# A scan between two dense layers: y of four sequences in one visit, sums on VectorE, scans between w and gT

## Chip, cores, metric

One core of one Trainium2 chip. The metric is the device time of one launch in microseconds, median of repeated launches; all runs used here are in the undisturbed state (granted TensorE clock 0.998 to 1.0). A *ratio* is the mean time of one kernel's fast runs over the mean of the other kernel's fast runs of the same rounds, so it is not quite the ratio of the medians that are quoted.

## The reference

A chunked state-space scan feeds a two-layer network with gate h cos(h):

```python
# batch 4, heads 8, sequence 768, head_dim 32, state 16
for c in range(nc):                          # chunks
    cum = np.cumsum(log_a[chunk])
    L   = np.exp(cum_i - cum_j) * causal
    y   = (C B^T * L) @ x  +  (C @ state) * exp(cum)
    state = decay_full * state + sum_j(B_j x_j * decay_from_j)
x = y.transpose(0, 2, 1, 3).reshape(3072, 256)
h = x @ w_in                                  # 256 -> 2048
out = (h * np.cos(h)) @ w_out                 # 2048 -> 256
```

All of it in fp32. The kernel makes chunks of 128 positions, so there are six (0 to 5), and 16 *turns* per chunk: one turn takes 256 columns of w_in for two of the four sequences, gates the result and multiplies it by w_out.

## The kernel before

Turn n of the loop issues the first product of turn n and the second product of turn n - 2. While chunk c goes through the network, chunk c + 1 is scanned. The parts that matter here:

```python
def first(n):                       # TensorE -> ScalarE -> VectorE
    hp[n] = bank([P, TB], "hp", "h")              # PSUM ring of two
    ... 4 matmuls hp <- w_in, yT ...
    ACT.activation(k, hp[n], AF.Copy, bias=0.25, scale=INV_2PI)
    V.scalar_tensor_tensor(out=w, in0=hp[n], scalar=INV_2PI, in1=k, ...)
def gate(n):   ACT.activation(cos, cos, AF.Sin, ...)
def gated(n):
    V.tensor_tensor(out=gT[n], in0=hp.pop(n), in1=cos, op=ALU.mult)
    differ(n)                                     # three gd on GpSimd

def seven(n):                       # second product, seven matmuls o
    ...                             # on g and gd; two PSUM banks lo, hi
    if j < NJ - 1: return           # every eighth turn:
    ACT.copy(out=ps[:, 0:3], in_=o[c, u][0][:, 0:3])
    V.tensor_copy(out=ps[:, 3:7], in_=o[c, u][1])
    for dst, a_, b_ in (...four adds...):
        G.tensor_tensor(out=dst, in0=a_, in1=b_, op=ALU.add)

# scan of a chunk, for a pair u of two sequences:
#   decays  4 x lam (VectorE scan)   turn2   transposes tp, rT
#   intra2  products g on TensorE    masked  m = g * lam (VectorE)
#   finish2 y = state*rT + xr*m on TensorE, then s_ps, carry
TURN = (NF - 5, NF + 3)             # turns 11 and 19, counted from
                                    # the start of chunk c - 1
for n in range(NC * NF + LAG):
    first(n); turn2 for pairs(n); gate(n); ...; gated(n)
    second(n - LAG)
    intra2, masked  for pairs(n - 1);  masked for pairs(n - 2)
    finish2         for pairs(n - 3)
    decays          for halves_at(n);  reaches for pairs(n + 1)
```

The names in the profile lines: hp is the first product of a turn in PSUM, w its phase and then its cosine, gT the gated result, gd three differences of blocks of gT that the second product o also takes, lam the decays, m the decayed products of the scan. A *y visit* is a stretch in which TensorE leaves the turns for the small matmuls of one scan step (y, then s_ps). A *sum turn* is one that ends an accumulator: ps copies it out of PSUM and four adds make the sums. A chunk is scanned while the chunk before it goes through the network, and a turn number below 16 given for a chunk (turn 2 of chunk 3) counts from the start of that stretch; sum turns are 1 and 9.

Of the kernel before, what the change touches and what calls it, by code (L numbers as in the profile page):

```python
# [8 lines left out]
FP32 = mybir.dt.float32  # L9
# [3 lines left out]
ALU = mybir.AluOpType  # L13
# [12 lines left out]
def kernel(  # L26
# [32 lines left out]
    NB, H, S, D = x.shape  # L59
    N = B.shape[-1]  # L60
    P = 128
    NC = S // P
# [26 lines left out]
    def pair(name):  # L89

        return psum.tile([P, 2, 4 * P], FP32, tag="scan", bufs=2, name=name)
# [142 lines left out]
    unit = const.tile([P, HH, P], FP32, name="unit")  # L234
    G.tensor_copy(out=unit, in_=ident.unsqueeze(1).to_broadcast([P, HH, P]))

    unit0 = const.tile([P, H, W], FP32, name="unit0")
    for t in range(2):
        ts = slice(t * W, (t + 1) * W)
        V.tensor_copy(out=unit0[ts], in_=ident[ts, ts].unsqueeze(1).to_broadcast([W, H, W]))  # L240
# [30 lines left out]
                    axis=mybir.AxisListType.XY, op=ALU.add)  # L271


    a0s = const.tile([P, 2, H, W], FP32, name="a0s")
    halves = a0z.rearrange("p (t i) -> p t i", t=2)
    for h in range(HH):
        ACT.activation(a0s[:, :, h], halves, AF.Copy, scale=mine[:, h:h + 1])
    for t in range(2):
        G.tensor_tensor(out=a0s[:, t, HH:H], in0=halves[:, t:t + 1].to_broadcast([P, HH, W]),
                        in1=mine[:, HH:H].unsqueeze(2).to_broadcast([P, HH, W]), op=ALU.mult)  # L280
    tos = const.tile([P, H, W], FP32, name="tos")
    G.tensor_tensor(out=tos, in0=to.unsqueeze(1).to_broadcast([P, H, W]),
                    in1=mine.unsqueeze(2).to_broadcast([P, H, W]), op=ALU.mult)

# [83 lines left out]
    def intra(b):  # L368
        bT, cT = part[0, b]
        g = [pair("g") for _ in range(2)]  # L370
        for q in range(4):
            r = slice(32 * q, 32 * q + 32)
            PE.matmul(g[q // 2][:, q % 2, 0:2 * P], lhsT=bT[r],
                      rhs=cT[r].rearrange("p t (s i) -> p s t i", s=2), start=True, stop=True)
        l = lam.pop((0, b))
        m = scan.tile([P, 2, H, W], FP32, tag="m", name="m")
        for q in range(2):
            of = [t[:, :, q * HH:(q + 1) * HH].rearrange("p s (k t) i -> p k s (t i)", k=2)
                  for t in (m, l)]
            V.tensor_tensor(out=of[0], in0=g[q][:, :, 0:2 * P].rearrange(  # L380
                "p k (s i) -> p k s i", s=2), in1=of[1], op=ALU.mult)
        part[0, b] = m
# [16 lines left out]
    def turn2(c, u):  # L399
        bc = raw[c][0]  # L400

        tp = pair("tp")[:, 0].rearrange("p (s k i) -> p s k i", s=2, k=2)
        for s in range(2):
            for k in range(2):
                PE.transpose(tp[:, s, k],  # L405
                             bc[:, k, heads(2 * u + s)].rearrange("p h n -> p (h n)"), ident)
        bT = scan.tile([P, 2, P], FP32, tag="bT2", bufs=1, name="bT2")
        ACT.copy(out=bT, in_=tp[:, :, 0])
        cT = scan.tile([P, 2, 2, P], FP32, tag="cT2", bufs=1, name="cT2")
        for t in range(2):  # L410
            ACT.activation(cT[:, :, t], tp[:, :, 1], AF.Copy, scale=slot[:, t:t + 1])
        rT = scan.tile([P, 2, P], FP32, tag="rT", bufs=1, name="rT")
        V.tensor_tensor(out=rT, in0=tp[:, :, 1], in1=reach[c, u], op=ALU.mult)
        part[c, u] = [bT, cT, rT]

# [10 lines left out]
    def masked(c, b):  # L426

        u, s = divmod(b, 2)
        g, ms = part[c, u][0:2]
        l = lam.pop((c, b))  # L430
        m = scan.tile([P, H, P], FP32, tag="m", name="m")
        for q in range(2):
            of = [t[:, q * HH:(q + 1) * HH].rearrange("p (k t) i -> p k (t i)", k=2)
                  for t in (m, l)]
            V.tensor_tensor(out=of[0], in0=g[q][:, :, s * 2 * P:(s + 1) * 2 * P], in1=of[1],  # L435
                            op=ALU.mult)
        ms.append(m)

    def finish2(c, u):
        (_, ms, rT), xr = part.pop((c, u)), raw[c][1]  # L440
        y = pair("y")


        for s in range(2):
            for q in range(4):
                r, p = slice(32 * q, 32 * q + 32), 64 * (q % 2)
                PE.matmul(y[p:p + 64, q // 2, s * P:(s + 1) * P],  # L447
                          lhsT=state[c - 1, u][r, s].rearrange("p t d -> p (t d)"),
                          rhs=rT[r, s], start=(s == 0), stop=False, tile_position=(32 * q, p),
                          skip_group_check=True)  # L450
        for s in range(2):
            for h in range(H):
                q, t = h % 4, h // 4
                PE.matmul(y[32 * q:32 * q + 32, t, s * P:(s + 1) * P], lhsT=xr[:, 2 * u + s, h],  # L454
                          rhs=ms[s][:, h], start=False, stop=True, tile_position=(0, 32 * q),
                          skip_group_check=True)
        if u == 0:
            yT[c] = two.tile([P, 2, TB], FP32, tag="yT", name="yT")
        ACT.copy(out=yT[c][:, :, 2 * u * P:(2 * u + 2) * P], in_=y[:, :, 0:2 * P])
        if c < NC - 1:  # L460
            s_ps = pair("s_ps")[:, 0, 0:4 * D].rearrange("p (s d) -> p s d", s=2)
            for s in range(2):
                sum_up(c, 2 * u + s, s_ps[:, s])
            carry(c, u, s_ps)

    def sum_up(c, b, s_ps):

        xr, sc = raw[c][1], scaled.pop((c, b))
        for q in range(4):
            two_ = slice(2 * q, 2 * q + 2)  # L470
            PE.matmul(s_ps[32 * q:32 * q + 32], lhsT=sc[:, two_].rearrange("p h n -> p (h n)"),
                      rhs=xr[:, b, two_].rearrange("p h d -> p (h d)"), start=True, stop=True,
                      tile_position=(0, 32 * q), skip_group_check=True)
# [51 lines left out]
    def gated(n):  # L525
        cos = turns.pop(n)
        gT[n] = ffn.tile([P, TB], FP32, tag="gT", bufs=LAG + 1, name="gT")
        V.tensor_tensor(out=gT[n], in0=hp.pop(n), in1=cos, op=ALU.mult)  # L528
        gT[n] = gT[n].rearrange("p (q m) -> p q m", q=4)
        if NF <= n < NC * NF - 1:  # L530
            differ(n)
# [49 lines left out]
    def seven(n):  # L581
# [38 lines left out]
        for dst, a_, b_ in ((sum_[:, 0:2], ps[:, 1:3], ps[:, 0:1]),  # L620
                            (sum_[:, 5:7], ps[:, 3:5], sum_[:, 0:1]),
                            (sum_[:, 3:5], ps[:, 5:3:-1], sum_[:, 5:6]),
                            (sum_[:, 2:3], ps[:, 6:7], sum_[:, 6:7])):
            G.tensor_tensor(out=dst, in0=a_, in1=b_.to_broadcast([P, dst.shape[1], P]), op=ALU.add)  # L624
        for s in range(2):
            nc.sync.dma_start(out=to_rows[2 * u + s, c],
                              in_=sum_[s * W:(s + 1) * W, 1:5].rearrange(
# [56 lines left out]
    for dst, src in ((a_cut, cut), (a_all, la)):  # L684
# [13 lines left out]
                 NF + 1: [(0, hind), (1, hind)], NF + 3: [(2, hind), (3, hind)]}  # L698


    TURN = (NF - 5, NF + 3)

    halves_of = {u: [(t - 4 + i, 2 * u + i // 2, i % 2) for i in range(4)]
                 for u, t in enumerate(TURN)}
    ahead = {1: {0: [(4, 0, 0), (6, 0, 1), (8, 1, 0), (9, 1, 1)]}}

    sums = {}

# [18 lines left out]

    def pairs(n):

        at = [(1 + (n - t) // NF, u) for u, t in enumerate(TURN) if (n - t) % NF == 0]  # L730
        return [(c, u) for c, u in at if 0 < c < NC]

    def halves_at(n):
        return [(c, b, t) for c in range(1, NC) for u in range(2)
                for m, b, t in ahead.get(c, {}).get(u, halves_of[u]) if m + (c - 1) * NF == n]

    EARLY = 3
    rest_of_loads()
    for n in range(NC * NF + LAG):
        c, f = divmod(n, NF)  # L740
        early = n < EARLY
        if n < NC * NF:
            if f == 0 and c > 0:
                load(c + 2)
            first(n)
            if n == 0:
                first_scan()
            for at in pairs(n):
                turn2(*at)
            rests = [grade(*piece[m], later=True)  # L750
                     for m in ((n,) if early else ()) + ((n + 1,) if n >= EARLY - 1 else ())
                     if m in piece]
            gate(n)
            for rest in rests:
                if rest:
                    rest()
            if not early and n in piece:
                join(*piece[n])
            gated(n)
            if early and n in piece:  # L760
                join(*piece[n])
            if n in (1, 2):
                carry(0, n - 1, sums[n - 1])
        for i, js in differ_at.get(n, ()):
            differ_w(i, js)
        if n >= LAG:
            second(n - LAG)
        for c, u in pairs(n - 1):
            intra2(c, u)
            masked(c, 2 * u)  # L770
        for c, u in pairs(n - 2):
            masked(c, 2 * u + 1)
        for c, u in pairs(n - 3):
            finish2(c, u)
            if u == 1:
                raw.pop(c)
        for c, b, t in halves_at(n):
            decays(c, b, t)
            if t == 1:
                load_a(c + 1, (b,))  # L780
        for c, u in pairs(n + 1):
            for b in (2 * u, 2 * u + 1):
                reaches(c, b)
                load_along(c + 1, (b,))
# [30 lines left out]
```

## Time and profile before

| | before |
|---|---|
| time, median | 386.46 us (386.18 to 387.12) |
| span of the profiled run | 384.9 us |
| busy: TensorE, VectorE, GpSimd, ScalarE | 98, 69, 64, 45% |
| from hp of turn 24 to hp of turn 40 (16 turns, one chunk) | 60.61 us |
| turn without scan work | 3.29 us |

The lines of the profile that the argument rests on stand in the prediction below.

### The profile page before, as it was taken

To read this page: it belongs to the slowest core of one execution; us is meant where nothing else is said; L and a number is where in the kernel's file an instruction comes from. 1 tells how busy PE (TensorE), PEld (TensorE's weight loads), DVE (VectorE), ACT (ScalarE), POOL (GpSimd) and SP (SyncE) were. 2 spreads that over 40 slices of the span, in tenths; PEclk is the share of its full clock that TensorE was granted. 3 is DMA by queue.
4 is the path that set the end of the run, shared out by engine and by line. 5 is a ranking of instruction groups with operands and counts; after the bars stand their busy time and mean duration, and the time that the engine had idled before them with its cause. 6 is when DMAs were issued, how large, how long until landed. Compare 5 with 4: busy or idle time off the path is not lost.

```text
span 384.9 us, 7726 instructions
## 1 busy us (share of the span) xinstructions
PE 378.3 (98%) x2982; PEld 331.2 (86%) x2982; DVE 265.9 (69%) x395; ACT 172.9 (45%) x303; POOL 245.4 (64%) x366
## 2 busy tenths in 40 slices
PE   8999999999999999999999999999999999999996
PEld 3578887888899899899899899899899989989995
DVE  7879999678667658657657757756765865863443
ACT  3878566534334334335334434434433433433441
POOL 5757665458859549648648837855955855853751
PEclk9999999999999999999999999999999999999999
DMA  7989899975002951301791301201210000010001
GB/s 83 270 235 266 249 230 137 181 96 151 2 0 63 148 52 57 96 2 54 127 81 55 97 2 56 81 17 43 68 43 1 21 10 0 2 27 3 7 22 27
DMA packets 106371, 30.42 MB, mean 79 GB/s; under 512 B 75520, under 2 KB 102240, under 8 KB 106336
## 3 DMA queue, kind: packets, MB, share of 16 engines
q1 hardware_dynamic: 106176, 29.81, 38.9%
q8 instruction: 23, 0.38, 0.5%
q10 hardware_dynamic: 160, 0.13, 0.1%
q14 instruction: 12, 0.10, 0.1%
HBM read 26.59 MB, written 3.34 MB: 78 GB/s over the span
## 4 chain that ended last, share of the span: by engine, by line
PE 82%; DVE 7%; POOL 3%; ACT 2%; issue 2%; DMA 2%; SPq 1%; ACTq 0%
PE hp L512 37%; PE o L609 32%; PE g L422 3%; PE y L454 3%; DVE mag L209 2%; DVE w L518 2%; DMA xr<-in_x_dram 2%; PE y L447 2%; DVE lam L344 2%; PE o L571 1%; DVE gT L528 1%; PE warm L101 1%; ACT w L523 1%; PE a_ps L298 1%; PE tp L405 1%
## 5 line engine op out<-in xcount | busy, mean ns | idle before, releaser
L512 PE MATMUL hp<-yT,w_in 128*128 128x256 f32 x768 | 184.4, 383 | 0.6 <-POOL w_in L217 0.3
L512 PEld LDWEIGHTS hp<-yT,w_in 128*128 128x128 f32 x768 | 139.2, 190 | 22.7 <-issue 4.5
L553 POOL TENSOR_TENSOR gd<-gT 128x256 f32<-128x256 f32 x79 | 71.9, 911 | 89.5 <-DVE gT L528 86.2
L528 DVE TENSOR_TENSOR gT<-hp,w 128x512 f32<-128x512 f32 x96 | 66.3, 691 | 69.9 <-ACT w L523 60.1
L523 ACT ACTIVATE w<-w,quarter 128x512 f32<-128x512 f32 x96 | 69.3, 722 | 97.2 <-DVE w L518 97.2
L516 ACT ACTIVATE k<-hp 128x512 int32<-128x512 f32 x96 | 57.1, 595 | 90.8 <-PE hp L512 90.7
L518 DVE SCALAR_TENSOR_TENSOR w<-hp,k 128x512 f32<-128x512 f32 x96 | 65.4, 681 | 36.7 <-ACT k L516 36.4
L609 PE MATMUL o<-words,gd 128*128 128x128 f32 x474 | 67.0, 277 | 0.6 <-POOL gd L555 0.6
L609 PEld LDWEIGHTS o<-words,gd 128*128 128x128 f32 x474 | 59.3, 192 | 2.4 <-POOL gd L555 2.2
L344 DVE TENSOR_TENSOR_SCAN lam<-arow,unit 128x512 f32<-128x512 f32 x40 | 55.7, 1394 | 0.0
L609 PEld LDWEIGHTS o<-w_out,gT 128*128 128x128 f32 x316 | 46.9, 191 | 3.6
L609 PE MATMUL o<-w_out,gT 128*128 128x128 f32 x316 | 48.0, 274 | 0.0
L555 POOL TENSOR_TENSOR gd<-gT,gd 128x128 f32<-128x128 f32 x79 | 43.1, 546 | 6.2
L556 POOL TENSOR_TENSOR gd<-gT,gd 128x128 f32<-128x128 f32 x79 | 35.9, 455 | 6.2
L571 PE MATMUL o<-w_out,gT 128*128 128x256 f32 x128 | 30.3, 380 | 0.4 <-POOL w_out L217 0.4
L609 PE MATMUL o<-w_out,gd 128*128 128x128 f32 x158 | 30.6, 275 | 0.0
L609 PE MATMUL o<-words,gT 128*128 128x128 f32 x158 | 30.5, 275 | 0.0
L571 PEld LDWEIGHTS o<-w_out,gT 128*128 128x128 f32 x128 | 24.2, 190 | 4.0 <-POOL w_out L217 0.8
L435 DVE TENSOR_TENSOR m<-g,lam 128x512 f32<-128x512 f32 x40 | 25.6, 681 | 0.0
L624 POOL TENSOR_TENSOR sum<-ps,sum 128x256 f32<-128x256 f32 (+1 forms) x27 | 24.2, 909 | 1.4
L609 PEld LDWEIGHTS o<-w_out,gd 128*128 128x128 f32 x158 | 24.0, 192 | 0.0
L609 PEld LDWEIGHTS o<-words,gT 128*128 128x128 f32 x158 | 24.0, 192 | 0.0
(91 smaller groups left out, 293.9 us busy)
## 6 DMA issues: line engine op xcount, KB each, us to landing
arow<-a_cut SPq DMA_DIRECT2D x20, 512.0 KB
words<-in_moe_w_in_dram SPq DMA_DIRECT2D x8, 512.0 KB
words<-in_moe_w_out_dram SPq DMA_DIRECT2D x8, 512.0 KB
out_dram<-sum SPq DMA_DIRECT2D x18, 128.0 KB
xr<-in_x_dram SPq DMA_DIRECT2D x4, 512.0 KB
along<-a_all SPq DMA_DIRECT2D x20, 64.0 KB
xr<-in_x_dram SPq DMA_DIRECT2D x8, 128.0 KB
bc<-in_B_dram SPq DMA_DIRECT2D x4, 256.0 KB
```

The source lines that it names most:

```text
L344: V.tensor_tensor_scan(out=lam[c, b][:, hs].rearrange("p h i -> p (h i)"), data0=rows_.rearrange("p h i -> p (h i)"), data1=unit.rearrange ...
L435: V.tensor_tensor(out=of[0], in0=g[q][:, :, s * 2 * P:(s + 1) * 2 * P], in1=of[1], op=ALU.mult)
L512: PE.matmul(to_[:, e], lhsT=w_in[:, k, fs], rhs=y[:, k, u], start=(k == 0), stop=(k == KT - 1), skip_group_check=True)
L516: ACT.activation(k, hp[n], AF.Copy, bias=0.25, scale=INV_2PI)
L518: V.scalar_tensor_tensor(out=w, in0=hp[n], scalar=INV_2PI, in1=k, op0=ALU.mult, op1=ALU.subtract)
L523: ACT.activation(cos, cos, AF.Sin, bias=quarter, scale=TWO_PI)
L528: V.tensor_tensor(out=gT[n], in0=hp.pop(n), in1=cos, op=ALU.mult)
L553: G.tensor_tensor(out=d[:, 0:2], in0=g[:, 1:2].to_broadcast([P, 2, P]), in1=g[:, 3::-3], op=ALU.subtract)
L555: G.tensor_tensor(out=d[:, 2], in0=g[:, 0], in1=d[:, 0], op=ALU.subtract)
L556: G.tensor_tensor(out=d[:, 3], in0=g[:, 2], in1=d[:, 2], op=ALU.subtract)
L571: PE.matmul(o[c, u][:, t], lhsT=g[:, 2 * e + t], rhs=w_out[:, 2 * j + e], start=(j == e == t == 0), stop=(j == NJ - 1 and e == 1), skip_gr ...
L609: PE.matmul(at[q], lhsT=a_[q], rhs=w[q], start=(j == 0 and q in starts), stop=(j == NJ - 1), skip_group_check=True)
```

## The change

The intent: (1) for chunks 2 to 5 compute y of all four sequences in one visit to TensorE instead of two; (2) take the four sums of a finished accumulator from GpSimd to VectorE; (3) issue scans (and the second m of a pair) between w and gT, where VectorE waits for the cosine. Larger buffer rings for m and rT make (1) possible; two setup tiles were put into the m ring to pay for it.

```diff
-    def finish2(c, u):
+    def finish2(c, us):                      # us = (0, 1) for chunks 2 to 5
+        parts = [(2*u + s, part[c,u][1][s], part[c,u][2][:, s]) for u in us for s in range(2)]
         y = pair("y")
-        for s in range(2):                   # state part, then m part
+        for i, (b, _, rT) in enumerate(parts):
 ...
-            G.tensor_tensor(out=dst, in0=a_, in1=b_..., op=ALU.add)
+            V.tensor_tensor(out=dst, in0=a_, in1=b_..., op=ALU.add)
 ...
-    TURN = (NF - 5, NF + 3)
+    late = [((0,), {0: 11}, [(4,0,0), (6,0,1), (8,1,0), (9,1,1)], 14),
+            ((1,), {1: NF + 2}, [(NF - 2 + i, 2 + i//2, i % 2) for i in range(4)], NF + 5)]
+    at_once = (0, 1), {0: 7, 1: 11}, 14      # transposes in turns 7, 11; y after 14
+    halves_of = {2: [(2,0,0), (3,0,1), (5,1,0), (6,1,1), (7,2,0), (8,2,1), (10,3,0), (11,3,1)]}
+    each = [(i - 1, i // 2, i % 2) for i in range(2 * NB)]   # scans in turns -1 to 6
 ...
+            behind = [halved(...) for halves_at(n)]
+            behind = [masked(c, 2u + 1) for pairs(n - 2)] + behind
+            if n not in piece and behind:    # from turn 16 on
+                behind.pop(0)()              # between w and gT
             gated(n)
+            for do in behind:
+                do()
```

More of the change, by code (lines that the diff above doesn't have):

```diff
@@ L235 @@
     G.tensor_copy(out=unit, in_=ident.unsqueeze(1).to_broadcast([P, HH, P]))
-    unit0 = const.tile([P, H, W], FP32, name="unit0")
+    both = scan.tile([P, 2, H, W], FP32, tag="m", bufs=4, name="both")
+    unit0, tos = both[:, 0], both[:, 1]
     for t in range(2):
@@ L271 @@
                     axis=mybir.AxisListType.XY, op=ALU.add)
-    a0s = const.tile([P, 2, H, W], FP32, name="a0s")
+    a0s = scan.tile([P, 2, H, W], FP32, tag="m", bufs=4, name="a0s")
     halves = a0z.rearrange("p (t i) -> p t i", t=2)
@@ L280 @@
                         in1=mine[:, HH:H].unsqueeze(2).to_broadcast([P, HH, W]), op=ALU.mult)
-    tos = const.tile([P, H, W], FP32, name="tos")
     G.tensor_tensor(out=tos, in0=to.unsqueeze(1).to_broadcast([P, H, W]),
@@ L375, in intra @@
         l = lam.pop((0, b))
-        m = scan.tile([P, 2, H, W], FP32, tag="m", name="m")
+        m = scan.tile([P, 2, H, W], FP32, tag="m", bufs=4, name="m")
         for q in range(2):
@@ L411, in turn2 @@
             ACT.activation(cT[:, :, t], tp[:, :, 1], AF.Copy, scale=slot[:, t:t + 1])
-        rT = scan.tile([P, 2, P], FP32, tag="rT", bufs=1, name="rT")
+        rT = scan.tile([P, 2, P], FP32, tag="rT", name="rT")
         V.tensor_tensor(out=rT, in0=tp[:, :, 1], in1=reach[c, u], op=ALU.mult)
@@ L430, in masked @@
         l = lam.pop((c, b))
-        m = scan.tile([P, H, P], FP32, tag="m", name="m")
+        m = scan.tile([P, H, P], FP32, tag="m", bufs=4, name="m")
         for q in range(2):
@@ L437, in masked @@
         ms.append(m)
-    def finish2(c, u):
-        (_, ms, rT), xr = part.pop((c, u)), raw[c][1]
+    def finish2(c, us):
+        xr = raw[c][1]
+        parts = [(2 * u + s, part[c, u][1][s], part[c, u][2][:, s]) for u in us for s in range(2)]
         y = pair("y")
-        for s in range(2):
+        for i, (b, _, rT) in enumerate(parts):
             for q in range(4):
                 r, p = slice(32 * q, 32 * q + 32), 64 * (q % 2)
-                PE.matmul(y[p:p + 64, q // 2, s * P:(s + 1) * P],
-                          lhsT=state[c - 1, u][r, s].rearrange("p t d -> p (t d)"),
-                          rhs=rT[r, s], start=(s == 0), stop=False, tile_position=(32 * q, p),
+                PE.matmul(y[p:p + 64, q // 2, i * P:(i + 1) * P],
+                          lhsT=state[c - 1, b // 2][r, b % 2].rearrange("p t d -> p (t d)"),
+                          rhs=rT[r], start=(i == 0), stop=False, tile_position=(32 * q, p),
@@ L450, in finish2 @@
                           skip_group_check=True)
-        for s in range(2):
+        for i, (b, m, _) in enumerate(parts):
             for h in range(H):
                 q, t = h % 4, h // 4
-                PE.matmul(y[32 * q:32 * q + 32, t, s * P:(s + 1) * P], lhsT=xr[:, 2 * u + s, h],
-                          rhs=ms[s][:, h], start=False, stop=True, tile_position=(0, 32 * q),
+                PE.matmul(y[32 * q:32 * q + 32, t, i * P:(i + 1) * P], lhsT=xr[:, b, h],
+                          rhs=m[:, h], start=False, stop=True, tile_position=(0, 32 * q),
@@ L456, in finish2 @@
                           skip_group_check=True)
-        if u == 0:
-            yT[c] = two.tile([P, 2, TB], FP32, tag="yT", name="yT")
-        ACT.copy(out=yT[c][:, :, 2 * u * P:(2 * u + 2) * P], in_=y[:, :, 0:2 * P])
+        s_ps = pair("s_ps")[:, 0].rearrange("p (u s d) -> p u s d", u=2, s=2)
+        for i, u in enumerate(us):
+            del part[c, u]
+            if u == 0:
+                yT[c] = two.tile([P, 2, TB], FP32, tag="yT", name="yT")
+            ACT.copy(out=yT[c][:, :, 2 * u * P:(2 * u + 2) * P],
+                     in_=y[:, :, 2 * i * P:(2 * i + 2) * P])
+            for s in range(2 if c < NC - 1 else 0):
+                sum_up(c, 2 * u + s, s_ps[:, u, s, 0:2 * D])
@@ L460, in finish2 @@
         if c < NC - 1:
-            s_ps = pair("s_ps")[:, 0, 0:4 * D].rearrange("p (s d) -> p s d", s=2)
-            for s in range(2):
-                sum_up(c, 2 * u + s, s_ps[:, s])
-            carry(c, u, s_ps)
+            for u in us:
+                carry(c, u, s_ps[:, u, :, 0:2 * D])
     def sum_up(c, b, s_ps):
@@ L623, in seven @@
                             (sum_[:, 2:3], ps[:, 6:7], sum_[:, 6:7])):
-            G.tensor_tensor(out=dst, in0=a_, in1=b_.to_broadcast([P, dst.shape[1], P]), op=ALU.add)
+            V.tensor_tensor(out=dst, in0=a_, in1=b_.to_broadcast([P, dst.shape[1], P]), op=ALU.add)
         for s in range(2):
@@ L698 @@
                  NF + 1: [(0, hind), (1, hind)], NF + 3: [(2, hind), (3, hind)]}
-    TURN = (NF - 5, NF + 3)
-    halves_of = {u: [(t - 4 + i, 2 * u + i // 2, i % 2) for i in range(4)]
-                 for u, t in enumerate(TURN)}
-    ahead = {1: {0: [(4, 0, 0), (6, 0, 1), (8, 1, 0), (9, 1, 1)]}}
+    late = [((0,), {0: 11}, [(4, 0, 0), (6, 0, 1), (8, 1, 0), (9, 1, 1)], 14),
+            ((1,), {1: NF + 2}, [(NF - 2 + i, 2 + i // 2, i % 2) for i in range(4)], NF + 5)]
+    at_once = (0, 1), {0: 7, 1: 11}, 14
+    halves_of = {2: [(2, 0, 0), (3, 0, 1), (5, 1, 0), (6, 1, 1), (7, 2, 0), (8, 2, 1), (10, 3, 0),
+                     (11, 3, 1)]}
+    each = [(i - 1, i // 2, i % 2) for i in range(2 * NB)]
+    plan = [(c, NF * (c - 1), *v) for c in range(1, NC) for v in (
+        late if c == 1 else [(*at_once[:2], halves_of.get(c, each), at_once[2])])]
     sums = {}
@@ L728, in pairs, with halved, ends @@
     def pairs(n):
-        at = [(1 + (n - t) // NF, u) for u, t in enumerate(TURN) if (n - t) % NF == 0]
-        return [(c, u) for c, u in at if 0 < c < NC]
+        return [(c, u) for c, at, _, turn_at, _, _ in plan for u in turn_at
+                if at + turn_at[u] == n]
     def halves_at(n):
-        return [(c, b, t) for c in range(1, NC) for u in range(2)
-                for m, b, t in ahead.get(c, {}).get(u, halves_of[u]) if m + (c - 1) * NF == n]
+        return [(c, *h) for c, at, _, _, halves_of, _ in plan for m, *h in halves_of if at + m == n]
+    def halved(c, b, t):
+        decays(c, b, t)
+        if t == 1:
+            load_a(c + 1, (b,))
+    def ends(n):
+        return [(c, us) for c, at, us, _, _, end in plan if at + end == n]
     EARLY = 3
@@ L758 @@
                 join(*piece[n])
+            behind = [lambda at=at: halved(*at) for at in halves_at(n)]
+            behind = [lambda at=(c, 2 * u + 1): masked(*at) for c, u in pairs(n - 2)] + behind
+            if n not in piece and behind:
+                behind.pop(0)()
             gated(n)
+            for do in behind:
+                do()
             if early and n in piece:
@@ L770 @@
             masked(c, 2 * u)
-        for c, u in pairs(n - 2):
-            masked(c, 2 * u + 1)
-        for c, u in pairs(n - 3):
-            finish2(c, u)
-            if u == 1:
+        for c, us in ends(n):
+            finish2(c, us)
+            if 1 in us:
                 raw.pop(c)
-        for c, b, t in halves_at(n):
-            decays(c, b, t)
-            if t == 1:
-                load_a(c + 1, (b,))
         for c, u in pairs(n + 1):
```

## The prediction

> **What bounds the kernel now.** I read the page's totals first, then the waits, then the order of time around one stage.
>
> ```profile
> span 384.9 us, 7726 instructions
> PE 378.3 (98%) x2982; PEld 331.2 (86%) x2982; DVE 265.9 (69%) x395; ACT 172.9 (45%) x303; POOL 245.4 (64%) x366
> PE 82%; DVE 7%; POOL 3%; ACT 2%; issue 2%; DMA 2%; SPq 1%; ACTq 0%
> ```
>
> TensorE sets the time. VectorE and GpSimd have a third of the span free; they matter only where TensorE waits for them. So I ask what TensorE's queue loses. The waits, with who waited, for whom, the total, the count and the longest:
>
> ```profile
> PEld o L609 <- POOL gd L555: 2.2, 9, 0.8
> PEld hp L512 <- issue: 4.5, 14, 0.6
> PEld y L454 <- issue: 1.7, 10, 0.2
> PEld o L609 <- DVE ps L619: 0.2, 1, 0.2
> ```
>
> In order of time, the starts of single matmuls lie on a fixed grid: a quiet turn (hp, then the seven products o) takes 1.73 + 1.56 = 3.29 us and repeats to 0.01 us. Off the grid after 90 us are only (a) the scan visits, (b) eight waits of 0.25 to 0.31 us (2.06 in all, a 0.10 us slow restart included) for a difference gd of GpSimd, each in the o three turns after the sums begin to be made, (c) one such wait of 0.82 us at 94 us behind GpSimd's weight differences, (d) one of 0.28 us at 209 us for VectorE's copy of an accumulator. (b) in chunk 3, from the timeline (start, length):
>
> ```profile
> 181.19 2.87 POOL L624 TENSOR_TENSOR sum<-ps,sum 128x256 f32<-128x256 f32 x3
> 181.68 1.32 DVE L344 TENSOR_TENSOR_SCAN lam<-arow,unit 128x512 f32<-128x512 f32 x1
> 184.02 0.84 POOL L553 TENSOR_TENSOR gd<-gT 128x256 f32<-128x256 f32 x1
> 185.45 0.74 PEld L609 LDWEIGHTS o<-words,gd 128*128 128x128 f32 x6 [0.18 <-POOL gd L555]
> ```
>
> The sums keep GpSimd until 184.02, gd comes late, and TensorE waits at 185.45. A y visit, ten of which exist:
>
> ```profile
> 194.30 0.39 PE L609 MATMUL o<-w_out,gd 128*128 128x128 f32 x2
> 194.62 0.67 PE L447 MATMUL y<-rT,state 32*64 32x128 f32 x16
> 195.21 1.08 PE L454 MATMUL y<-m,xr 128*32 128x128 f32 x32
> 196.11 0.41 PE L471 MATMUL s_ps<-xr,sc 128*32 128x64 f32 x16
> 196.44 0.48 PE L512 MATMUL hp<-yT,w_in 128*128 128x256 f32 x1
> ```
>
> And a quiet turn of VectorE with a scan after gT:
>
> ```profile
> 199.17 0.69 DVE L518 SCALAR_TENSOR_TENSOR w<-hp,k 128x512 f32<-128x512 f32 x1 [2.11 <-ACT k L516]
> 200.72 0.69 DVE L528 TENSOR_TENSOR gT<-hp,w 128x512 f32<-128x512 f32 x1 [0.86 <-ACT w L523]
> 201.32 1.22 DVE L344 TENSOR_TENSOR_SCAN lam<-arow,unit 128x512 f32<-128x512 f32 x1
> 201.55 1.51 POOL L553 TENSOR_TENSOR gd<-gT 128x256 f32<-128x256 f32 x1 [3.11 <-DVE gT L528]
> ```
>
> VectorE idles 0.86 us between w and gT, waiting for ScalarE's cosine; gd takes 1.51 us beside the scan, 0.73 elsewhere.
>
> **What the Trainium skill says.** "Perfetto Trace Analysis", Identifying the Most-Contended Engine, warns that matmul busy time does not show how near TensorE is to its limit, and names weight-load time and MFU instead; so I use starts, not the 98%. "TensorEngine Tiling (Array Packing)", Key Properties: switching the tiling mode drains the array. The trace agrees: 205 ns from the last o to the first y against 112 within o, 198 ns from the row-tiled to the column-tiled part against 109 within each, 320 ns between the first two hp afterwards against 216. "SBUF — State Buffer", Who interferes with whom: a VectorE instruction with two SBUF inputs and a GpSimd instruction that reads SBUF exclude each other. The trace agrees (gd 0.73 alone, 1.51 beside a scan); copies and products that read PSUM, such as ps and m, leave gd at 0.73.
>
> **The change part by part.**
>
> (1) One y visit instead of two for chunks 2 to 5. Streaming is kept: groups of four small matmuls every 109 ns (y) and 56 ns (s_ps). Saved is what one visit pays apart from its groups, read from single starts: entry 205 - 112 = 93; first state group 161 - 109 = 52; switch 217 - 109 = 108; first group of the m part 133 - 109 = 24; end of s_ps 169 - 56 = 113; slow second hp 320 - 216 = 104. Sum 0.49 us; four times, 1.98 us off the path. The transposes (tp) and g are still two visits. Chunk 1 keeps its two y visits, because its data come during chunk 0.
>
> (2) The sums go to VectorE. GpSimd loses 9 x (0.73 + 2.87) = 32 us, off the path apart from the eight waits: -2.06 us. VectorE gains 9 x four adds. It has the same forms at the end of the kernel: 0.425 us for 128x256, 0.293 for 128x128, with some 0.03 between dependent ones: 3 x 0.46 + 0.33 = 1.7 us, 15 us in all. Since they have two SBUF inputs, they alternate with the three gd of the turn. With w at 2.62 us after the start of its hp, gT at 4.17 to 4.41 and ps 0.6 later, I get the end of the sums at 7.4 to 7.65 us after that hp. The next w would start at 5.9, so it is 1.5 to 1.7 late.
>
> (3) A scan between w and gT. w issues in 0.60, the scan takes some 1.15, so gT starts 1.75 to 1.8 us after w in place of 1.55: 0.25 later, but GpSimd's gd no longer collides with the scan. TensorE needs gT two turns on, when hp's bank is reused: 6.58 us after hp in quiet turns, gT now ending at 4.86. The slack is 1.72 us, so most turns cost nothing.
>
> (4) Two places where this slack is used up. Where a sum turn also has a scan or a product m before gT (7 of 9), ps ends near 5.69 in place of 5.45; TensorE writes the second of the two accumulator banks again at 5.69. With 0.05 for the semaphore and 0.10 for the restart that is 0.15 us, 7 times: +1.05 us. In the turn after a sum, where there is a scan too (chunks 3 to 5, turn 2, three times), gT ends near 4.15 + 1.75 + 0.69 = 6.6 against 6.58: about 0.16 each, +0.48 us. Where transposes lie in between (turn 10) the limit is 7.02 and nothing is lost.
>
> (5) Moves. In chunk 1 the second half's transposes come a turn earlier, and its g lies before the o that waited at 94 us: GpSimd has 1.43 us more there. I expect this wait (0.82) gone, and the one at 209 us (0.28) too, or counted among the seven of (4). The larger rings for m and rT and the two setup tiles put into the m ring change no wait on the path: up to turn 13 the order on every engine is the same, so the first 70 us should be equal, the 0.4 us wait at 60.5 included.
>
> Sum: -1.98 - 2.06 - 0.82 - 0.28 + 1.05 + 0.48 = -3.61 us. The median before is 386.46, so **382.8 us**, 0.9% less; the span near 381.3.
>
> **The rivals.** *VectorE becomes the bound in places.* For it: in chunks 2 to 5 all scans, products and sums fall into some eleven turns, where a turn holds w 0.6, scan 1.15, gT 0.6 and often 1.2 to 1.7 more, against 3.29; the two tightest turns have a margin of nothing. Against it: the backlog of a sum is worked off at 0.9 us a turn in the turns after. If each of 18 sums and reach turns missed by 0.2 us, it would cost 3.6 us: about 386.4, the whole gain. *The wait for gd stays,* because VectorE's sums block GpSimd in place of its own: for it, 1.51 against 0.73 us; against it, the three gd need 1.4 us and alternate with the sums, ending near 7.0 us after hp against a need of 6.58 + 1.73 + 0.45 = 8.76 for the second. It would leave 384.9. *Everything works and the restarts of (4) don't come:* 386.46 - 5.14 = 381.3. *The y visit saves nothing* because the matmuls wait for the last m: against it, the last m is made in turn 13 and the visit follows turn 14; this would give 384.8.
>
> **Range and chances.** 381.3 is the floor of what I can find, and 384.8 the sum with one of the two large terms lost. I take **381.3 to 384.8**. Faster by over 2% would need 7.7 us, more than all waits on the path: 0.02. Slower by over 2% would need steady stalls of VectorE, 0.1 us in every turn and more: 0.02. Within 2%: 0.96.
>
> **What would show it.** Right: six y visits instead of ten, a merged one some 3.5 us from its first y to the next hp; no wait of o for gd L555; GpSimd busy 245 - 32 = 213 us or less, VectorE near 266 + 15 = 281; gd about 0.73 in most turns; scans of chunks 2 to 5 in the idle time before gT; small waits of o for the copy ps about every 8 turns. Wrong: waits of hp for gT in turns 2, 3, 10 or 11 of the chunks, longer than 0.2 us; a lasting wait for gd; or a start (first 70 us) that differs, which I took as equal.

## The result

| | before | changed |
|---|---|---|
| time, median | 386.79 us (386.18 to 387.15, 4 runs) | 382.71 us (382.49 to 383.33, 4 runs) |
| ratio, 95% interval | | 0.9899 (0.988 to 0.9918) |
| span of the profiled run | 384.9 us | 381.3 us |
| period, turn 24 to 40 | 60.61 us | 60.04 us |

Later the same changed kernel gave 0.9906 and 0.9921. The gain is about 1%. The totals of the changed kernel's page (busy time, share, instructions):

```profile
span 381.3 us, 7681 instructions
PE 375.1 (98%) x2982; PEld 330.9 (87%) x2982; DVE 279.1 (73%) x431; ACT 172.2 (45%) x303; POOL 213.5 (56%) x330
```

VectorE has 13 us more, GpSimd 32 us less, TensorE the same instructions. In the changed kernel's waits no o waits for a gd any more; GpSimd idles longer before its first gd instead (103.5 us in all, 89.5 before), and TensorE waits for none of that:

```profile
POOL gd L560 <- DVE gT L535: 74.3, 48, 4.6
POOL gd L560 <- PE hp L519: 25.4, 13, 3.0
```

The joined y visit of the changed kernel (lines are 7 lower in its text, so y is L450 and L457):

```profile
134.37 0.39 PE L616 MATMUL o<-w_out,gd 128*128 128x128 f32 x2
134.69 1.10 PE L450 MATMUL y<-rT,state 32*64 32x128 f32 x32
135.72 1.95 PE L457 MATMUL y<-m,xr 128*32 128x128 f32 x64
137.49 0.63 PE L478 MATMUL s_ps<-xr,sc 128*32 128x64 f32 x32
138.05 0.91 PE L519 MATMUL hp<-yT,w_in 128*128 128x256 f32 x3
```

From first y to hp it takes 3.36 us; by single starts the single visit before took 1.83, twice 3.66. With the entry (0.09) and the slow second hp (0.10), which are outside these numbers, the difference is 0.49 us.

And a turn of the changed kernel that has both a scan and the sums (turn 33), with the turn after it:

```profile
147.35 0.69 DVE L525 SCALAR_TENSOR_TENSOR w<-hp,k 128x512 f32<-128x512 f32 x1 [0.64 <-ACT k L523]
147.96 1.24 DVE L345 TENSOR_TENSOR_SCAN lam<-arow,unit 128x512 f32<-128x512 f32 x1
149.12 0.66 DVE L535 TENSOR_TENSOR gT<-hp,w 128x512 f32<-128x512 f32 x1
149.70 0.67 DVE L626 COPY ps<-o 128x512 f32<-128x512 f32 x1
150.30 0.63 DVE L631 TENSOR_TENSOR sum<-ps 128x256 f32<-128x256 f32 x1
150.96 1.36 DVE L631 TENSOR_TENSOR sum<-ps,sum 128x256 f32<-128x256 f32 x3
152.25 0.68 DVE L525 SCALAR_TENSOR_TENSOR w<-hp,k 128x512 f32<-128x512 f32 x1
152.85 1.21 DVE L345 TENSOR_TENSOR_SCAN lam<-arow,unit 128x512 f32<-128x512 f32 x1
153.98 0.66 DVE L535 TENSOR_TENSOR gT<-hp,w 128x512 f32<-128x512 f32 x1
154.78 0.89 PE L519 MATMUL hp<-yT,w_in 128*128 128x256 f32 x3
```

VectorE has no pause from 147.35 to the second gT. hp of turn 33 starts at 144.73, so ps ends at 144.73 + 5.64 and the sums at 144.73 + 7.6; the second gT ends at 154.64 and hp of turn 36, which uses its bank again, starts at 154.78, 0.07 off the grid. This is the place where the slack is used up. The other kind of place is a sum turn in which VectorE has a product m or a scan before gT (here turn 25, in which two m run until 117.48):

```profile
118.00 0.68 DVE L626 COPY ps<-o 128x512 f32<-128x512 f32 x1
118.44 1.00 PE L616 MATMUL o<-words,gd 128*128 128x128 f32 x6
```

The copy of the accumulator ends at 118.68 and the first o that writes this bank again starts at 118.73, so that these six matmuls take 1.00 us where they take 0.83 on the grid.

### The profile page after: what moved, and what is told of

Same layout as the page of the kernel before. It is cut to its first block, busy times and chain, and to the rows that moved or that the text cites. A ratio compares the mean times of both kernels' runs of the same rounds, so it can differ in the third digit from the quotient of the medians.

```text
span 381.3 us, 7681 instructions
## 1 busy us (share of the span) xinstructions
PE 375.1 (98%) x2982; PEld 330.9 (87%) x2982; DVE 279.1 (73%) x431; ACT 172.2 (45%) x303; POOL 213.5 (56%) x330
## 4 chain that ended last, share of the span: by engine, by line
PE 87%; DVE 6%; ACT 2%; issue 2%; POOL 1%; ACTq 0%
PE hp L519 40%; PE o L616 33%; PE g L423 3%; PE o L578 3%; PE y L457 3%; DVE mag L209 2%; PE y L450 1%; DVE w L525 1%; DVE gT L535 1%; PE warm L101 1%; DVE mag L207 1%; PE tp L406 1%; PE a_ps L299 1%; ACT w L530 1%; DVE lam L345 1%
## 5 line engine op out<-in xcount | busy, mean ns | idle before, releaser
L560 POOL TENSOR_TENSOR gd<-gT 128x256 f32<-128x256 f32 x79 | 59.4, 752 | 103.5 <-DVE gT L535 74.3
L535 DVE TENSOR_TENSOR gT<-hp,w 128x512 f32<-128x512 f32 x96 | 65.1, 678 | 33.3 <-ACT w L530 30.7
L563 POOL TENSOR_TENSOR gd<-gT,gd 128x128 f32<-128x128 f32 x79 | 46.0, 582 | 6.2
L562 POOL TENSOR_TENSOR gd<-gT,gd 128x128 f32<-128x128 f32 x79 | 42.7, 541 | 6.2
L328 POOL TENSOR_TENSOR sc<-bc,lam 128x128 f32<-128x128 f32 x20 | 8.5, 431 | 14.7 <-DVE lam L345 7.3
```

The costliest lines, as they stand in the source:

```text
L560: G.tensor_tensor(out=d[:, 0:2], in0=g[:, 1:2].to_broadcast([P, 2, P]), in1=g[:, 3::-3], op=ALU.subtract)
L562: G.tensor_tensor(out=d[:, 2], in0=g[:, 0], in1=d[:, 0], op=ALU.subtract)
L563: G.tensor_tensor(out=d[:, 3], in0=g[:, 2], in1=d[:, 2], op=ALU.subtract)
```

## The experiments

Each kernel was compared with the kernel before on the same chip in five rounds. *Period* is from hp of turn 24 to hp of turn 40, and from 40 to 56 and 56 to 72, where they differ.

| kernel | ratio to before | period, us |
|---|---|---|
| before | 1 | 60.61, 60.96, 60.61 |
| changed (three measurements) | 0.9899, 0.9906, 0.9921 | 60.04 |
| a1 changed, sums on GpSimd | 1.0007 | 61.91, 61.70, 60.74 |
| a2 before, sums on VectorE | 1.0078 | 61.29 |
| a3b changed, scans behind sums | 1.0064 | 62.51, 61.24, 61.25 |
| a4 two visits, turns 13 and 14 | 1.0029 | 61.19 |
| a4b two visits, turns 14 and 15 | 0.9971 | 60.52 |
| a5 chunk 1 a turn later | 0.9944 | 60.04 |
| b1 free sum turns, first try | 0.9889 | 59.77 |
| c1 free sum turns | 0.9879, 0.9868 | 59.62 |

**a0: the changed kernel again**, no edit.

> The changed kernel itself once more, as the measure for the others of this call: about 382.7 us, span 380.5 to 381.3, waits of TensorE after 90 us about 1.4 us in all.

383.06 us (382.76 to 383.36), ratio 0.9906, span 380.7 us: as expected. A third measurement beside a5 and c1:

> The changed kernel as the measure for these two: period 60.04 us, ratio to the kernel before near 0.990.

383.51 us, ratio 0.9921 (0.9908 to 0.9935), period 60.05. The three ratios differ by 0.002 for one and the same kernel, so ratios of different calls should not be compared below that; the period can.

**a1: the sums alone back on GpSimd.**

```diff
-            V.tensor_tensor(out=dst, in0=a_, ...
+            G.tensor_tensor(out=dst, in0=a_, ...
```

> The changed kernel with the four sums back on GpSimd, all else kept. Theory 1 (the sums' own place is worth the 2.06 us that I credited to it): the eight waits of o for gd come back, the waits of hp for gT in turn 2 (0.43 us) go: 1.6 us more than the changed kernel, about 384.3. Rival (gd was late because sums, gd and scans excluded each other, and the scans' new place before gT alone frees GpSimd): no wait for gd, or only in turn 10 where the two reach scans still collide (up to 4 times 0.25): between 0.5 less and 0.5 more than the changed kernel.

386.89 us, ratio 1.0007 (0.999 to 1.0024): the whole gain is gone, 3.8 us, over twice what theory 1 had said. The rival falls, and so does the size. The trace shows why; GpSimd and TensorE of a1 from turn 34 on:

```profile
152.46 0.72 POOL L631 TENSOR_TENSOR sum<-ps 128x256 f32<-128x256 f32 x1
153.26 2.87 POOL L631 TENSOR_TENSOR sum<-ps,sum 128x256 f32<-128x256 f32 x3
154.44 1.44 DVE L345 TENSOR_TENSOR_SCAN lam<-arow,unit 128x512 f32<-128x512 f32 x1
156.09 0.41 POOL L328 TENSOR_TENSOR sc<-bc,lam 128x128 f32<-128x128 f32 x1
156.46 0.72 POOL L560 TENSOR_TENSOR gd<-gT 128x256 f32<-128x256 f32 x1
157.77 0.74 PEld L616 LDWEIGHTS o<-words,gd 128*128 128x128 f32 x6 [1.13 <-POOL gd L562]
157.80 1.39 POOL L563 TENSOR_TENSOR gd<-gT,gd 128x128 f32<-128x128 f32 x1
159.24 0.30 PEld L616 LDWEIGHTS o<-w_out,gd 128*128 128x128 f32 x2 [0.51 <-POOL gd L563]
```

With a scan before gT in every turn from -1 to 6, the sums on GpSimd meet a scan, the sc product and the next scan. gd of turn 34 starts at 156.46, 3.6 us after its gT was done (152.83), and o waits twice. That chunk loses 1.9 us (period 61.91 against 60.04), the next 1.7 and the third 0.7; from first hp to last matmul a1 takes 4.2 us longer than a0. So with the sums on GpSimd, o waits 2.06 us for gd in the old order of turns, but 4.6 us in the new one (both with restarts).

**a2: the kernel before with nothing but the sums moved.**

```diff
-            G.tensor_tensor(out=dst, in0=a_, ...      # before.py
+            V.tensor_tensor(out=dst, in0=a_, ...
```

> The kernel before with nothing changed but the four sums on VectorE. If the sums' place were worth its 2.06 us by itself: 2.06 us less than before, about 384.7. Theory now (the parts depend on each other: here the scan stands behind the sums in the sum turn, so w of the next turn comes 1.9 us later and gT passes the limit of 7.02 us after hp): waits of hp for gT of about 0.5 us and of o for gd of about 0.5 us in each half chunk, 5 us more than before rather than less.

389.3 us, ratio 1.0078 (1.0064 to 1.0092): 3.0 us slower, 2.5 to 3.6 by the interval, and 2.4 us from first hp to last matmul in the traces. The eight waits for gd after the sums are gone, as my sum has it, but a wait of hp for gT takes the place of each. VectorE and TensorE of a2:

```profile
148.43 1.36 DVE L624 TENSOR_TENSOR sum<-ps,sum 128x256 f32<-128x256 f32 x3
149.71 1.21 DVE L344 TENSOR_TENSOR_SCAN lam<-arow,unit 128x512 f32<-128x512 f32 x1
150.84 0.66 DVE L518 SCALAR_TENSOR_TENSOR w<-hp,k 128x512 f32<-128x512 f32 x1
152.37 0.69 DVE L528 TENSOR_TENSOR gT<-hp,w 128x512 f32<-128x512 f32 x1 [0.86 <-ACT w L523]
153.20 1.10 PE L512 MATMUL hp<-yT,w_in 128*128 128x256 f32 x4 [0.35 <-DVE gT L528]
```

Sums and then a scan stand in front of the next w; VectorE afterwards idles 0.86 us for the cosine, and gT is late for hp. Each costs 0.59 us with the restart against 0.25 saved; eight times 0.34, less the 0.28 us wait for ps that went too, is the 2.4 us of the traces. The wait that I expected for gd did not come, so it is not 5. The same move that carries the change loses time when done alone.

**a3b: scans and second m behind the sums.**

```diff
-            if n not in piece and behind:
-                behind.pop(0)()
             gated(n)
-            for do in behind: do()
 ...
             second(n - LAG)
+        for do in behind: do()
```

> The changed kernel with the scans and second m products behind gT, the copy ps and the sums, where the kernel before has them. Theory (VectorE's order in a turn decides): the waits for ps go (1.0 us), but in turns 2 and 10 gT ends near 7.5 us after its hp against limits of 6.58 and 7.02: about 1 us in turn 2 of chunks 3 to 5 and 0.5 us in turn 10, in all 3 to 5 us more than the changed kernel, 386 to 388. Rival (VectorE is idle for over a quarter of the span, its order inside a turn does not matter; what helped was only to relieve GpSimd): within 0.5 us of the changed kernel.

388.76 us, ratio 1.0064 (1.0051 to 1.0077). Lines of VectorE and TensorE from the sums of turn 33 on:

```profile
152.63 1.36 DVE L631 TENSOR_TENSOR sum<-ps,sum 128x256 f32<-128x256 f32 x3
153.91 1.21 DVE L345 TENSOR_TENSOR_SCAN lam<-arow,unit 128x512 f32<-128x512 f32 x1
155.04 0.66 DVE L525 SCALAR_TENSOR_TENSOR w<-hp,k 128x512 f32<-128x512 f32 x1
156.57 0.69 DVE L535 TENSOR_TENSOR gT<-hp,w 128x512 f32<-128x512 f32 x1 [0.86 <-ACT w L530]
157.41 0.89 PE L519 MATMUL hp<-yT,w_in 128*128 128x256 f32 x3 [0.72 <-DVE gT L535]
```

It is some 6 us more than the changed kernel by the ratios (1.0064 - 0.9906) and by the trace (6.1 us more from first hp to last matmul): the theory's mechanism, but more than its 3 to 5 us. hp waits 0.89 us for gT after turn 2 and 0.60 after turn 10, where 1 and 0.5 were expected. What my figure left out are single waits around chunk 2, where the scans of two chunks meet: two y visits that waited 0.65 and 0.49 us, an o that waited 0.7 us for the accumulators' copies, and one more late gT (0.74). VectorE was busy 72% here, no more than in the changed kernel; its order inside a turn decides.

**a4 and a4b: two y visits again.** First after turns 13 and 14:

```diff
-        return [(c, us) for c, at, us, _, _, end in plan if at + end == n]
+        return [(c, (u,)) for c, at, us, _, _, end in plan for u in us
+                if at + end - us[-1] + u == n]
```

> The changed kernel with the y visit of chunks 2 to 5 made twice again (sequences 0 and 1 after turn 13, 2 and 3 after turn 14), same streaming. Theory (a visit has a fixed price of 0.49 us on TensorE, from single starts): 1.98 us more, about 384.7. Rival (the gain came from elsewhere, joining is neutral): within 0.3 us of the changed kernel.

387.85 us, ratio 1.0029: more than either theory. The first visit waited 0.67 us in each chunk, because y takes the PSUM buffer that the last m products read:

```profile
130.91 1.28 DVE L436 TENSOR_TENSOR m<-g,lam 128x512 f32<-128x512 f32 x2
131.74 0.67 PE L450 MATMUL y<-rT,state 32*64 32x128 f32 x16 [0.60 <-DVE m L436]
```

So this experiment measured two things at once. The second try puts the visits after turns 14 and 15 (`us[0]` for `us[-1]`):

> Two y visits for chunks 2 to 5 once more, now after turns 14 and 15, because in the first try the first visit waited 0.67 us per chunk for a PSUM buffer still read by the last m. Theory (fixed price of a visit 0.49 us): the period from hp of turn 24 to hp of turn 40 is 60.04 + 0.49 = 60.53 us and the time 2.0 us over the changed kernel, 384.7 to 385.0. Rival (the visit's price was only that wait): period within 0.1 us of 60.04.

385.2 us (384.72 to 385.84), ratio 0.9971 (0.9959 to 0.9984). The period is 60.52 us, 0.48 over the changed kernel, where 0.49 was expected. A visit has a fixed price; from turn 24 to turn 88 nothing else changed, and four chunks make 1.9 us. At the very end a4b has 0.37 us more, where the last o waits for the last gT (a4 has this too); why that gT came later was not traced.

**a5: the second half of chunk 1 a turn later**, as before the change.

```diff
-            ((1,), {1: NF + 2}, [(NF - 2 + i, ...)], NF + 5)]
+            ((1,), {1: NF + 3}, [(NF - 1 + i, ...)], NF + 6)]
```

> The changed kernel with the second half of chunk 1 a turn later throughout (scans 15 to 18, transposes after hp of turn 19, g after turn 20, y after turn 22), as in the kernel before. Theory (step 5: the wait of 0.82 us at 94 us went because g now lies ahead of the o that waited): the wait for gd in turn 20 comes back, 0.8 us more between hp of turn 14 and hp of turn 24 than in the changed kernel, apart from the moved visits. Rival (it went because scans ahead of gT leave GpSimd free for its weight differences): no wait there, or under 0.2 us.

384.41 us, ratio 0.9944 (0.9931 to 0.9958), beside 0.9921 for the changed kernel in the same call. The stretch from hp of turn 14 to hp of turn 24 took 40.85 us, 1.10 more than in the changed kernel. In the waits of a5 it stands as

```profile
PEld o L616 <- POOL gd L562: 0.6, 1, 0.6
PEld o L616 <- POOL gd L563: 0.4, 1, 0.4
```

With scans ahead of gT and g behind the o, the wait is back and even a little longer. And in a3b, where the scans stand behind gT but g lies ahead, no o waited there. So it was the place of g.

**b1 and c1: sum turns without scan or m.** The first try moves two scans out of turns 1 and 2 and makes both m of a pair right after g:

```diff
-    each = [(i - 1, i // 2, i % 2) for i in range(2 * NB)]
+    each = [(t, i // 2, i % 2) for i, t in enumerate((-1, 0, 3, 4, 5, 6, 7, 8))]
-            behind = [masked(c, 2u + 1) for pairs(n - 2)] + behind
 ...
             masked(c, 2 * u)
+            masked(c, 2 * u + 1)
```

> A version meant to beat both: in chunks 3 to 5 the scans go to turns -1, 0, 3 to 8 (none in turns 1 and 2), and both m of a pair are made right after g, in turns 8 and 12 (none before gT in turns 9 and 13). Theory (the 1.43 us left are the waits for the copy ps in turns 1 and 9 and for gT in turn 2, because VectorE has work before gT in the sum turns): all of them gone, 1.4 us less than the changed kernel, about 381.3. Rival (VectorE is full there, and the work moved brings the same waits into turns 8 to 11): within 0.4 us of the changed kernel.

382.62 us, ratio 0.9889. The waits in turns 1 and 2 were gone, but 0.15 us a chunk stayed: four m and a scan in turn 8 pushed w of turn 9 from 2.72 to 2.95 us after its hp. The period fell by 0.27 and not by 0.42, and the time is barely less than the changed kernel's. The second try keeps turn 8 free as well:

```diff
-    ... enumerate((-1, 0, 3, 4, 5, 6, 7, 8))
+    ... enumerate((-2, -1, 0, 3, 4, 5, 6, 7))
-    halves_of = {2: [(2,..), (3,..), (5,..), (6,..), (7,..), (8,..), (10,..), (11,..)]}
+    halves_of = {2: [(2,..), (3,..), (4,..), (5,..), (6,..), (7,..), (10,..), (11,..)]}
```

> The version with free sum turns once more, with the scans of chunks 3 to 5 in turns -2, -1, 0 and 3 to 7 and those of chunk 2 in turns 2 to 7, 10, 11, so that no scan lies in turn 8 either. In the first try 0.15 us a chunk was left because four m products and a scan in turn 8 pushed w of turn 9 back by 0.23 us. Theory: no wait of TensorE for ps or gT after turn 24, period 60.04 - 0.42 = 59.62 us, about 1.4 us under the changed kernel, near 381.6. Rival (a further wait hides behind this one): period 59.77 or more.

> The version with free sum turns again, beside the changed kernel on the same chip: period 59.62 us again; 1.4 us (0.37%) under the changed kernel.

381.65 us (381.39 to 382.19) and 381.44 us (381.12 to 382.69), ratios 0.9879 and 0.9868; in the second the changed kernel had 0.9921, so c1 is 0.5% faster than it (0.9868 / 0.9921; the traces make it 1.4 us from turn 24 to the last matmul, 267.15 against 268.6), and the results are correct. It beats both kernels. The period is 59.62 us in both, as expected to 0.01. The sum turn of c1:

```profile
148.21 0.69 DVE L535 TENSOR_TENSOR gT<-hp,w 128x512 f32<-128x512 f32 x1 [0.79 <-ACT w L530]
148.81 0.68 DVE L626 COPY ps<-o 128x512 f32<-128x512 f32 x1
149.41 0.64 DVE L631 TENSOR_TENSOR sum<-ps 128x256 f32<-128x256 f32 x1
150.09 1.36 DVE L631 TENSOR_TENSOR sum<-ps,sum 128x256 f32<-128x256 f32 x3
151.37 0.68 DVE L525 SCALAR_TENSOR_TENSOR w<-hp,k 128x512 f32<-128x512 f32 x1
152.91 0.69 DVE L535 TENSOR_TENSOR gT<-hp,w 128x512 f32<-128x512 f32 x1 [0.86 <-ACT w L530]
153.98 0.38 PE L519 MATMUL hp<-yT,w_in 128*128 128x256 f32 x1
```

hp of this turn starts at 144.11; ps ends 5.38 us after it, and the next gT 0.38 us before hp needs it. From turn 24 to the last step every start of TensorE lies on the grid except for the visits themselves. VectorE idles 0.79 us between w and gT of this turn, and this is right: here filling the gap costs more than leaving it.

## Why the prediction was right

The measured median lies 0.1 us from the forecast; the steps, with what the starts of single matmuls in the changed kernel show:

| step | predicted, us | measured, us | by |
|---|---|---|---|
| (1) four joined visits | -1.98 | -1.98 (traces), -1.9 | a4b |
| (2) eight waits for gd | -2.06 | -2.06, none left | waits, a1, a2 |
| (5) wait at 94 us | -0.82 | -0.82, none left | a5 |
| (5) wait for ps at 209 us | -0.28 | gone | trace |
| (4) waits for ps, seven | +1.05 | +1.00 (four of 0.17, three of 0.11) | c1 |
| (4) waits for gT in turn 2, three | +0.48 | +0.43 (0.14 each) | c1 |
| sum | -3.61 | -3.71 | |

From the first hp to the last matmul the two profiled runs differ by 3.75 us. The times differ by 4.08 in the first comparison and by ratios of 0.9906 and 0.9921, 3.6 and 3.1 us, in the later ones; the middle one is the forecast. So the agreement to 0.1 us is partly luck, the mechanism is not.

*The scan's new place (step 3)* was right in its cost: gT starts 1.77 us after w in turn 33 (149.12 - 147.35), forecast 1.75 to 1.8. That gd no longer collides with the scan is right only for the first gd of a turn: its mean in the profile went from 911 to 752 ns, and 2 of 79 took over 1 us where 17 did before. The collision mostly moved on to the third gd (582 ns on average, before 455). All gd together took 148.1 us, before 151.0. No o waits for the third one, so this had no effect on the time.

*VectorE and GpSimd totals:* forecast 281 and at most 213, measured 279.1 and 213.5. The four adds took 2.02 us beside the gd, not 1.7, but they ended 7.59 us after hp in turn 33, within the forecast 7.4 to 7.65. *The start:* forecast equal up to turn 13, whose hp starts 46.42 us after the first before the change and 46.39 after it; the wait at 60.5 us is there in both with 0.40 us.

*What the prediction did not see* is that its terms do not stand side by side. It booked 2.06 us for the sums and a few tenths for the order on VectorE. Done alone, the sums lose 3.0 us (a2); taken back alone, 3.8 us (a1); the order taken back alone costs about 6 us (a3b). Only both together give the -2.06 and leave +1.43. The prediction reckoned the final state turn by turn, so its sum holds; a reader who took single terms from it to decide which part to keep would have been wrong.

*The rivals.* VectorE as a bound came true in the two kinds of place that step 4 names, at 1.43 us and not 3.6, and c1 takes these waits away: shown. That gd would still wait, and that the y visit would wait for the last m, did not happen in the changed kernel; a4 shows that the second was not far (there y waits 0.67 us).

## What to carry to other kernels

Where one engine runs on a grid, measure the slack of each producer (when its result is ready, against when it is needed) and put work into turns by that slack, not by the engine's share of busy time: VectorE had 27% idle and still cost 1.4 us, because three kinds of work met in one turn. Moving work to another engine and reordering that engine's queue can each lose time and gain together, so test them in both combinations. Joining two visits of small tiled matmuls saves a fixed price per visit, which can be read from the starts around one visit before anything is built.

## What the Trainium skill lacked or had wrong

- "TensorEngine Tiling (Array Packing)", Key Properties, says that a change of tiling mode drains the array, but gives no price. Here a visit with two modes cost 0.49 us apart from its streaming (0.48 by a4b): 93 ns at entry, 108 between the modes, 104 at the second full matmul after it, the rest at first and last groups.
- "SBUF — State Buffer", Who interferes with whom, has the exclusion of VectorE with two SBUF inputs and GpSimd right. It does not say that two series of short instructions then alternate: dependent adds of VectorE took 0.56 us each beside GpSimd's gd where the same form takes 0.425 alone (in turn 33 each add ended 0.28 us after a gd, each gd 0.31 after an add), and a GpSimd difference of 0.455 us that had waited out a scan ended 0.25 us after the scan (a1, 159.19 against 158.94), which suggests that part of its time runs while it waits.
- No page that I read has the restart of TensorE: the matmul that follows the one that waited starts a further 0.09 to 0.10 us late (o) or 0.075 us late (hp), at the waits of o and hp for other engines between 90 us and the last step in these traces.
- No page has the spread of the start: the first hp of one and the same kernel (c1) started at 18.1 us in one profiled run and at 19.3 in another, nearly as far apart as c1 and the changed kernel, so that spans of single runs cannot settle changes below 1 us here.
